# Which experts' first products are formed in blocks in the first batch, and the knobs of a hand-written schedule, on one Trainium2 core

## The chip, the core and the metric

The kernel runs on one core of one Trainium2 chip. The metric is the device time of one execution in microseconds (us); the median of several runs counts. A profiled execution has two numbers of its own: its device time, and its span, which goes from the first to the last instruction of the program.

## What is computed

Sliding-window attention with sink tokens is followed by a mixture of four experts over the same tokens. Cut to what matters:

```
q, k, v: [4 batches, 8 heads, 768 tokens, 64]      window 128, 4 sink tokens
a   = softmax(q k^T / 8), kept where key < 4 or 0 <= query - key < 128
x   = (a v), laid out as [3072 tokens, 512]
p   = domain_probs / (sum over experts + 1e-9)      [3072, 4]
out = sum over e of  p[:, e] * (relu(x @ w1[e]) @ w2[e])
w1: [4, 512, 1024]     w2: [4, 1024, 512]
```

## The kernel before

**Tiling.** A group is 256 tokens; each of the four batches has three. (b, g) is group g of batch b. A *unit* (b, g, e) is the first product of one group with one expert: x times w1[e], the relu, and, from (0, 2) on, the gate. A unit is made in one of three ways:

- *Plain* (`emit_first`, matmuls at L1114): four steps of eight matmuls, each 128x128 by 256 columns, so 32 matmuls of 256 columns. A step ends with one operation that takes the relu and writes half a block of H (L1127 on ACT, L1129 on DVE, or L1138 on DVE with the gate).
- *In blocks*, which the code calls fast (`emit_fast`, L1204): a product of 2x2 blocks with seven block products in place of eight (P1 to P7), so 56 matmuls of 128 columns. Its block sums cost ACT two copies of 128x512 (L1250, L1263) and DVE two additions of 128x512 (L1257, L1272) on top of the four relu or gate operations that a plain unit has too.
- *Turned* (`emit_turning`, L1316): the same seven block products with the operands exchanged, 14 matmuls of 512 columns. The result lies the wrong way round and is turned by two DMA transposes into H.

A unit in blocks needs, besides the tokens, four sums of blocks of w1[e] (`weight_form1`, L390 to L396, one DVE operation of 128x1024 each) and four sums of token blocks of its group (`tokens`, L1170). The last of the four weight sums overwrites a block of w1[e], so it waits until no plain unit of that expert is left.

`START` says from which (b, g) on an expert's units are made in blocks: expert 2 always, expert 1 from (0, 2), experts 0 and 3 from (1, 0). So batch 0 has four units in blocks and eight plain ones. The 20 units from (2, 1) on are turned.

The second product is plain for (0, 0) and (0, 1) (`emit_second`, L1575, eight matmuls of 512 columns for 128 tokens and one expert) and in seven block products after that (`emit_product`, L1489), again with sums on DVE (L1430, L1407).

**What sets the order.** All instructions are written out in order by a planner that runs while the program is built. It keeps a clock for each engine (`t["pe"]`, `t["dve"]`, ...) and for the DMA queue, with a cost for each operation. In each round it lists what TensorE could do next (an attention step, a step of an open unit, a second product), when each is ready by these clocks and with which priority, and emits the best. Operations of ACT and DVE are put on a list by `later` with the time at which they are ready and a slack (`MASK`, `FORM`, `TOKEN`, ...); of those that are ready, the one with the earliest deadline is emitted first. So a slack moves an operation in DVE's queue, and any change of a cost or of a readiness can reorder everything that follows.

**Weights, rows and homes.** Weights and the rows of q, k and v come in by DMAs that POOL issues in program order, through one queue. The first ones are written out by hand (L505 to L520); those of experts 1 and 2 are next; when the attention of batch 0 has been emitted, the loads of w1[3], w2[3] and of the rows of batch 1 are appended (L1678 to L1687). The planner starts the weight sums of an expert `MARGIN1` (4000 ns) after its estimate of when w1[e] has landed, and none before `SOON` while only batch 0 is under way (L1708); `next_form` asks for one at a time, experts in the order 0 to 3. Six homes hold H (`NH`); a second product of plain kind frees its home at its end, a product in blocks at its last block. Units of (0, 2) keep theirs until all second products of (0, 0) and (0, 1) are done. At most two units are open at a time (`WIDE`).

Of the kernel before, what the change touches and what calls it, by code (L numbers as in the profile page):

```python
# [12 lines left out]
BF16 = mybir.dt.bfloat16  # L13
# [3 lines left out]
def kernel(  # L17
# [57 lines left out]
    MASK = 5000  # L75
    GATE = 800
    GATE0 = 300
    FORM = 6000
    TOKEN = 3000
# [7 lines left out]
    SCALED = 300  # L87
    SHARED = 2
# [4 lines left out]
    SOON = 34000  # L93
    NEARLY = 2
    ROWED = 24000
    GATED = 38000
    W2AT = 2
# [411 lines left out]
    load_v(0, (2, 3))  # L509
    load_w1(0, 4, [0])  # L510
    load_w1(0, 4, [1])
# [235 lines left out]
    def values(b, hp, g):  # L747
# [6 lines left out]
        for qi in range(2):  # L754
            qb = 2 * g + qi
            terms = []
            c = 0
            for (kb, q0, nq) in GROUPS[g]:
                if q0 <= qb < q0 + nq:
                    terms.append((kb, c + (qb - q0) * P))  # L760
                c += nq * P
            if g > 0:
                nc.tensor.matmul(  # L763
                    od[:, qi], lhsT=sinkA[b][:, (qb - 2) * P:(qb - 1) * P], rhs=vsd[b][:, hp],
                    start=True, stop=False, skip_group_check=True,
                )
                cols += 2 * DX
            for ph in range(2):
                for i, (kb, c) in enumerate(terms):
                    nc.tensor.matmul(  # L770
                        od[:, qi, ph], lhsT=a[:, ph, c:c + P], rhs=vx[kb][:, 2 * hp + ph, 0:DX],
                        start=(g == 0 and i == 0), stop=(i == len(terms) - 1), skip_group_check=True,
                    )
                    cols += DX + 5
# [174 lines left out]
    NH = 6  # L949
# [6 lines left out]
    class Mixture:  # L956


        def __init__(self):
            self.early = {g: list(range(E)) for g in range(NEARLY)}  # L960
            self.open = []
            self.units = []
            for b, g in PAIRS:
                fast = [e for e in EXPERTS.get((b, g), range(E)) if self.is_fast(b, g, e)]
                slow = [e for e in range(E) if e not in fast]
                if b == 0:
                    fast, slow = list(range(E)), []
# [6 lines left out]
            self.turning = set(mine[TURNED_UNITS[0]:len(mine) - TURNED_UNITS[1]])  # L974
            self.gated = [u for u in self.order if u not in self.turning]
# [9 lines left out]
            self.stored, self.homed = [], False  # L985
            self.spare, self.lent = [], {}
# [7 lines left out]
        def room(self):  # L994
            if self.units and self.units[0] in self.turning and self.halves() < 2:
                return False
            return self.spare or self.live < NH
# [14 lines left out]
        def widened(self):  # L1012

            x = sb.tile([P, 2, NHP, S], BF16, name="qkT", tag="qkT", bufs=1)
            x = x.rearrange("p i h n -> p (i h n)")
            n = 2 * QF * 2 * P
            self.spare = [x[:, i * n:(i + 1) * n].rearrange("p (k f t n) -> p k f t n", k=2, f=QF, t=2) for i in range(3)]
            self.rest("onat", 2, 2, t["pe"])
            self.rest("aT", 4, 1, t["pe"])

        def opened(self, b, g, e):

            if self.spare:
                self.H[b, g, e] = self.spare.pop()
                self.lent[b, g, e] = self.H[b, g, e]
            else:
                self.H[b, g, e] = mo.tile([P, 2, QF, 2, P], BF16, name="H", tag="H", bufs=NH)
                self.live += 1
            fast = self.is_fast(b, g, e)
            if (b, g, e) in self.turning:  # L1030
                self.G[b, g, e] = [self.half(), self.half()]

            def complete(at):
                self.H_at[b, g, e] = at
                self.finished.add((b, g, e))
                if (b, g) >= PAIRS[0]:
                    self.waiting.append((b, g, e))
                    load_gates()
                    if not TURNED_UNITS[1] and self.gated[-1] == (b, g, e):
                        self.rest_gates()  # L1040

            self.H_part[b, g, e] = join(4, complete)
            return {"unit": (b, g, e), "fast": fast, "left": list(UNITS) if fast else list(range(QF)), "at": {}}
# [17 lines left out]
        def firsts(self):  # L1061
# [15 lines left out]
            if n < WIDE and self.units and (self.units[0][0] or loaded) and early <= MIX and self.room() and not (early + zero and self.live >= NH - 1):  # L1077
# [68 lines left out]
        def tokens(self):  # L1146
# [13 lines left out]
            B11, B21, B12, B22 = x[:, 1, 0:2], x[:, 1, 2:4], x[:, 0, 0:2], x[:, 0, 2:4]  # L1160
# [5 lines left out]
            self.T[b, g] = {"P1": B11, "P2": B21, "P3": B22, "P4": T[:, 3], "P5": T[:, 0], "P6": T[:, 1], "P7": T[:, 2]}  # L1166
            steps = [(T[:, 0], B12, B11), (T[:, 1], B22, T[:, 0]), (T[:, 2], B22, B12), (T[:, 3], B21, T[:, 1])]

            def run(engine):
                nc.vector.tensor_sub(*steps.pop(0))  # L1170
                done = dve(G, rate=1.92)
# [109 lines left out]
        def emit_turning(self, u, m, ready):  # L1281
            b, g, e = u["unit"]
            H, X, at = self.H[b, g, e], self.G[b, g, e], u["at"]
            n = QF * P
            assert len(own_steps) == 4
            if m in ("P1", "P5"):
                spare = [i for i in range(6) if ring[i] <= ready + 40]
                spare.sort(key=lambda i: (whole[i], ring[i]))
                if m == "P1":
# [5 lines left out]
                    def turned(k):  # L1295
                        def turn(at):
                            nc.sync.dma_start(
                                out=H[:, k].rearrange("c f t n -> c (f t) n"), in_=X[k].rearrange("p f t n -> p (f t n)"), transpose=True,
                            )
                            done = sp(at, issue=1330, takes=1400, turning=True) + LANDS  # L1300
                            self.H_part[b, g, e](done)
                            self.H_part[b, g, e](done)
                            self.resting.append((done, X[k]))
# [83 lines left out]
        def chore(self):  # L1387
# [12 lines left out]
            if self.last:  # L1400
                b, g, e = u = self.last[0]
                if (b, g, "P2") not in self.products:
                    self.last.pop(0)

                    def form(engine):
                        H12 = self.H[b, g, e][:, 1, :, 0]
                        nc.vector.tensor_sub(H12, H12, self.S[b, g][1][:, e])  # L1407
                        self.S4_at[u] = dve(QF * P, rate=1.92)
                    return go(form, self.until(b, g, e, "P3"))
# [9 lines left out]
            self.waiting.pop(0)  # L1419
            if (b, g) not in self.S:  # L1420
                self.S[b, g] = [mo.tile([P, E, QF, P], BF16, name=f"S{i}", tag=f"wide{i}", bufs=1) for i in range(2)]
            H = self.H[b, g, e]
            H11, H21, H22 = H[:, 0, :, 0], H[:, 0, :, 1], H[:, 1, :, 1]
            S = self.S[b, g]
            steps = [(nc.vector.tensor_add, S[0][:, e], H21, H22), (nc.vector.tensor_sub, S[1][:, e], S[0][:, e], H11),
                     (nc.vector.tensor_sub, H21, H11, H21)]

            def form(engine):
                x = steps.pop(0)
                x[0](*x[1:])  # L1430
                at = dve(QF * P, self.stored[-1] if (b, g) == PAIRS[0] else 0.0, rate=1.92)
                if steps:
                    go(form, self.until(b, g, e, "P6 P7".split()[len(steps) == 2]))
                else:
                    self.S_at[u] = at
                    self.last.append(u)
            return go(form, self.until(b, g, e, "P6"))
# [5 lines left out]
        def operand(self, b, g, e, m):  # L1443
            H = self.H[b, g, e]
            if m in ("P5", "P6"):
                return self.S[b, g]["P5 P6".split().index(m)][:, e]
# [23 lines left out]
        def emit_product(self):  # L1470
# [30 lines left out]
            if m == CHAIN[-1]:  # L1501
                if (b, g, e) in self.lent:
                    self.spare.append(self.lent.pop((b, g, e)))
                else:
                    self.live -= 1
# [56 lines left out]
        def emit_second(self):  # L1562
# [35 lines left out]
            if s == 1:  # L1598
                self.live -= 1
# [16 lines left out]
    def own_made():  # L1616
# [13 lines left out]
        later("dve", t["pe"], 5000, run)  # L1630
# [29 lines left out]
    while mix.more() or att.more():  # L1660
# [69 lines left out]
        opts.append((max(p, now), HIGH_PRODUCT if behind > BEHIND or mix.live >= FULL or wide and TURN_ABOUT and mix.turn_about else LOW_PRODUCT, "product", None))  # L1730
# [65 lines left out]
```

## Time and profile before

| | us |
|---|---|
| median of 3 runs | 354.03 (353.99 to 354.43) |
| the profiled execution, its own time | 354.08 |
| its span | 352.37 |
| TensorE's last matmul ends, from the start of the span | 349.20 |
| TensorE busy (matmuls) | 346.4 |
| VectorE (DVE) busy | 284.1 |
| ScalarE (ACT) busy | 207.9 |
| GpSimd (POOL) busy | 73.6 |

TensorE's granted clock is full throughout. Matmuls are pipelined: a matmul's listed duration holds its way through the array, so what it costs in a row of matmuls is the distance from its start to the next start. The chain of work that ended last is 94% TensorE.

### The profile page before, as it was taken

Reading aid. Unit: us, or ns where it says so; the run is one execution under the profiler, and the core shown is the slowest. Engines: PE = TensorE matmul, PEld = TensorE weight load, DVE = VectorE, ACT = ScalarE, POOL = GpSimd, SP = SyncE. Lnnn points to the kernel's source line nnn. Section 1 sums busy time; section 2 is a strip of 40 time slices with the busy share of each in tenths; the row PEclk is TensorE's granted clock in tenths of the full one; section 3 lists DMA queues with packets and bytes.
Section 4 is the critical chain, followed back from the end, with each engine's and each line's share of the span. In section 5 each row is a group of like instructions: output and inputs, shape, how many; then the busy total and the mean of one; then the engine's idle time right before and its main releaser. Section 6 shows DMA issues by size and latency. Waiting matters only on the chain.

```text
span 352.4 us, 9356 instructions
## 1 busy us (share of the span) xinstructions
PE 346.4 (98%) x3722; PEld 266.8 (76%) x3722; DVE 284.1 (81%) x673; ACT 207.9 (59%) x475; POOL 73.6 (21%) x91
## 2 busy tenths in 40 slices
PE   7999999999999999999999999999999999999996
PEld 3685769756789998998999886755856676666685
DVE  6886999978999999799898999578768586675740
ACT  6763723438775443647463439689579767666611
POOL 8966114340442606000152000000000000000000
PEclk9999999999999999999999999999999999999999
DMA  9999999999999999720999513646438743645541
GB/s 178 177 188 195 221 216 180 176 158 178 154 141 133 148 205 110 95 70 6 91 204 169 85 38 55 126 96 121 86 84 166 134 96 91 121 116 111 75 120 61
DMA packets 161032, 45.61 MB, mean 129 GB/s; under 512 B 144740, under 2 KB 156996, under 8 KB 160988
## 3 DMA queue, kind: packets, MB, share of 16 engines
q0 software_dynamic: 79104, 17.31, 56.0%
q1 hardware_dynamic: 80828, 27.18, 42.4%
q8 instruction: 29, 0.48, 0.6%
q10 hardware_dynamic: 1056, 0.52, 0.5%
q14 instruction: 15, 0.12, 0.1%
HBM read 38.39 MB, written 6.34 MB: 127 GB/s over the span
## 4 chain that ended last, share of the span: by engine, by line
PE 94%; DVE 3%; DMA 2%; POOL 0%; issue 0%; ACT 0%; DVEq 0%
PE acc L1489 35%; PE cps L1204 18%; PE cps L1316 17%; PE acc L1575 8%; PE hps L1114 7%; PE sps L704 3%; PE od L770 3%; DMA vx<-in_v_dram 2%; PE od L763 1%; DVE aT L738 1%; DVE T L1170 1%; DVE onat L800 1%; PE tx L834 1%; PE tr L601 0%; PE sinks L665 0%; PE acc L580 0%
## 5 line engine op out<-in xcount | busy, mean ns | idle before, releaser
L1489 PEld LDWEIGHTS <-H 128*128 128x128 bf16 x708 | 66.6, 98 | 17.8 <-issue 1.1
L729 ACT ACTIVATE aT<-sps 128x512 bf16<-128x512 f32 (+1 forms) x96 | 47.2, 579 | 16.7 <-PE sps L704 16.6
L1489 PE MATMUL acc<-w,H 128*128 128x256 bf16 x420 | 56.8, 273 | 0.0
L1204 PEld LDWEIGHTS <-w 128*128 128x128 bf16 x640 | 39.2, 98 | 1.2 <-issue 0.5
L1489 PEld LDWEIGHTS <-S 128*128 128x128 bf16 x320 | 30.4, 98 | 9.4 <-issue 0.8
L1237 DVE SCALAR_TENSOR_TENSOR H<-cps,gates 128x512 bf16<-128x512 f32 x54 | 36.4, 681 | 0.0
L1334 ACT ACTIVATE cps<-cps 128x512 f32<-128x512 f32 x44 | 25.5, 585 | 17.4 <-PE cps L1316 17.0
L1114 PE MATMUL hps<-xT,w 128*128 128x256 bf16 x256 | 31.9, 273 | 0.2 <-DVE H L1129 0.2
L815 ACT ACTIVATE onat<-od,R 128x64 bf16<-128x64 f32 x108 | 24.9, 324 | 11.4 <-DVE R L797 11.1
L315 POOL DMA_DIRECT2D vx<-in_v_dram x24 | 21.4, 898 | 45.1 <-PE od L770 34.0
L1204 PEld LDWEIGHTS <-vf 128*128 128x128 bf16 x480 | 29.3, 98 | 1.0 <-issue 0.5
L1575 PE MATMUL acc<-w,H 128*128 128x512 bf16 x128 | 29.9, 379 | 0.0
L1489 PE MATMUL acc<-wf,H 128*128 128x256 bf16 (+1 forms) x216 | 29.6, 272 | 0.0
L1114 PEld LDWEIGHTS <-w 128*128 128x128 bf16 x256 | 24.2, 98 | 4.9 <-issue 1.1
L1337 ACT ACTIVATE rest<-cps,own_gates 128x512 bf16<-128x512 f32 x37 | 25.5, 693 | 0.7
L723 DVE TENSOR_TENSOR aT<-aT,mask 128x1024 bf16<-128x1024 bf16 (+1 forms) x36 | 22.6, 637 | 3.1 <-ACT aT L729 2.9
L250 POOL DMA_DIRECT2D qkn<-in_q_dram x22 | 19.6, 893 | 25.7 <-DMA qkT<-qkn 18.1
L1204 PE MATMUL cps<-T,w 128*128 128x128 bf16 x320 | 24.3, 219 | 0.0
L1204 PE MATMUL cps<-xT,w 128*128 128x128 bf16 x320 | 24.1, 219 | 0.0
L1316 PE MATMUL cps<-w,T 128*128 128x512 bf16 x80 | 23.8, 379 | 0.0
L1316 PE MATMUL cps<-vf,T 128*128 128x512 bf16 x80 | 23.6, 379 | 0.0
L1550 ACT COPY osb<-acc 128x256 f32<-128x256 f32 x32 | 12.1, 381 | 19.3 <-PE acc L1489 19.1
(145 smaller groups left out, 676.6 us busy)
## 6 DMA issues: line engine op xcount, KB each, us to landing
w<-in_moe_w_dram POOLq DMA_DIRECT2D x6, 1024.0 KB, 18.5
out_dram<-osb SPq DMA_DIRECT2D x16, 256.0 KB
vx<-in_v_dram POOLq DMA_DIRECT2D x24, 128.0 KB, 6.7
qkn<-in_q_dram POOLq DMA_DIRECT2D x22, 128.0 KB, 6.9
qkn<-in_k_dram POOLq DMA_DIRECT2D x22, 128.0 KB, 7.1
gates<-gate_rows SPq DMA_DIRECT2D x20, 128.0 KB
w<-in_moe_w_dram POOLq DMA_DIRECT2D x4, 256.0 KB, 7.4
w<-in_moe_w_dram POOLq DMA_DIRECT2D x2, 512.0 KB, 10.8
```

Of the source, the lines that this page charges most:

```text
L315: nc.gpsimd.dma_start(out=vx[tb][:, :, 0:D], in_=v[b, :, tb * P:(tb + 1) * P, :].rearrange("h p d -> p h d"),)
L723: nc.vector.tensor_mul(a, a, m[:, None, :].to_broadcast([P, 2, w]))
L729: nc.scalar.activation(out=a[:, ph], in_=sps[ph][:, 0:w], func=AF.Exp, scale=scale)
L815: nc.scalar.mul(o[:, qi, hp, ph * D:(ph + 1) * D], od[:, qi, ph, 0:D], R[:, qi, ph])
L1114: nc.tensor.matmul(h[:, i].rearrange("p (q n) -> p q n", q=2), lhsT=w1_sb[e][:, db, fb * P:(fb + 1) * P], rhs=xT[b, g][:, :, db], start=(i ...
L1204: nc.tensor.matmul(y[:, f], lhsT=A[:, d, f * P:(f + 1) * P], rhs=T[:, d], start=(m in ("P1", "P5") and f == 0 and d == 0), stop=(d == 1), ...
L1237: nc.vector.scalar_tensor_tensor(out=dst, in0=src, scalar=0.0, in1=gate, op0=ALU.max, op1=ALU.mult)
L1316: nc.tensor.matmul(y.rearrange("p f n -> p (f n)"), lhsT=T[:, d], rhs=A[:, d], start=(m in ("P1", "P5") and d == 0), stop=(d == 1), skip_g ...
L1334: nc.scalar.activation(out=src, in_=src, func=AF.Relu)
L1337: nc.scalar.mul(X[k][:, :, s], src, gate)
L1489: nc.tensor.matmul(y, lhsT=self.operand(b, g, e, m)[:, f], rhs=forms[e][m][:, f, cs], start=(k == 0 and f == 0 and m in (("P1", "P5", "P2" ...
L1575: nc.tensor.matmul(op, lhsT=H[:, fb // QF, fb % QF, s], rhs=w2_sb[e][:, fb, :], start=(fb == 0), stop=(fb == NFB - 1),)
```

## The change

It does five things.

1. `START`: expert 1's units are in blocks from (1, 0) on, no longer from (0, 2); expert 3's from (0, 0) on, no longer from (1, 0). Batch 0 then has six units in blocks (experts 2 and 3) and six plain ones (experts 0 and 1).
2. The loads: the first quarter of w1[0] goes ahead of the last block of v of group (0, 1); w1[3] goes behind the first row block of batch 1 (`W1AT`).
3. The slacks of masks, weight sums and token sums are shorter, and `SOON` is 24000 in place of 34000.
4. From batch 1 on the two 128-token halves of a group change places in the attention's result, and the first two token sums become one operation of 512 columns.
5. The homes of H are one tile with a list of free places, the oldest first; a turned unit takes its home when its transpose is emitted, and counts against the free ones from when it is opened. The order of the rows in the S tiles is that in which the units are done. Expert gates for the turned units are loaded earlier, for batches 1 to 3, and normalised earlier. Other new names stand at values that switch them off (`EXTRA`, `PROMISED`, `JOIN`, `WAITS` at 0, `ALTER` with 99).

```diff
-    OWN = 2
-    TURNED_UNITS = (4, 0)
+    OWN = 1
+    TURNED_UNITS = (16, 0)
-    START = {0: (1, 0), 1: (0, 2), 2: (0, 0), 3: (1, 0)}
+    START = {0: (1, 0), 1: (1, 0), 2: (0, 0), 3: (0, 0)}
-    MASK = 5000
+    MASK = 4000
-    FORM = 6000
-    TOKEN = 3000
+    FORM = 4500
+    TOKEN = 2000
-    SOON = 34000
+    SOON = 24000
+    W1AT = 1
...
-    load_v(0, (2, 3))
+    load_v(0, (2,))
     load_w1(0, 4, [0])
+    load_v(0, (3,))
     load_w1(0, 4, [1])
...
-                    od[:, qi], lhsT=sinkA[b][...], rhs=vsd[b][:, hp],
+                    od[:, qi ^ (b > 0)], lhsT=sinkA[b][...], rhs=vsd[b][:, hp],
...
+            one, two = (0, 1) if b else (1, 0)
+            B11, B21, B12, B22 = x[:, one, 0:2], x[:, one, 2:4], x[:, two, 0:2], x[:, two, 2:4]
...
+            steps = [(T[:, 2], B22, T[:, 0]), (T[:, 3], B21, T[:, 2])]
+            if b:
+                steps = [(T[:, 0:2], x[:, 1].rearrange(...), x[:, :, 0:2])] + steps
+            else:
+                steps = [(T[:, 0], B12, B11), (T[:, 1], B22, B12)] + steps
...
-            self.spare, self.lent = [], {}
+            self.homes = [mo.tile([P, NH, 2, QF, 2, P], BF16, name="H", tag="H", bufs=1)]
+            self.spare += [(self.homes[0], i) for i in range(NH)]
...
+        def home(self, u):
+            self.lent[u] = x, i = self.spare.pop(0)
+            self.H[u] = x[:, i]
+            self.live += 1
...
             if (b, g, e) in self.turning:
                 self.G[b, g, e] = [self.half(), self.half()]
+                self.promised.append((b, g, e))
+            else:
+                self.home((b, g, e))
...
-            loads.append((load_w1, 3))
             for tb in range(NQB):
+                if tb == W1AT:
+                    loads.append((load_w1, 3))
                 if tb == W2AT:
                     loads.append((load_w2, 3))
                 loads.append((load_nat, 1, tb))
...
         if rowed == 1 and now > GATED:
             rowed = 2
             load_gates()
+            if OWN == 1:
+                own_load()
...
-            if ahead == 1:
+            if ahead == 1 and OWN > 1:
                 own_load()
-            elif ahead == 2:
-                own_made()
+            elif ahead == OWN:
+                own_made(0 if OWN > 1 else 20000)
```

More of the change, by code (lines that the diff above doesn't have):

```diff
@@ L1076, in firsts @@
                 yield at, (OPEN if n else 2), ("early", g)
-            if n < WIDE and self.units and (self.units[0][0] or loaded) and early <= MIX and self.room() and not (early + zero and self.live >= NH - 1):
+            if n < WIDE and self.units and (self.units[0][0] or loaded) and early <= MIX and self.room() and not (early + zero and self.free() <= 1):
                 yield self.unit_ready(*self.units[0], QF), (OPEN if n else 2) - EARLY, ("unit",)
@@ L1296, in turn @@
                         def turn(at):
[L1297 to L1303, printed above, removed]
+                            self.unturned.append(((b, g, e), k, at))
+                            self.turn_rows(True)
                         return join(2, turn)
@@ L1403, in chore @@
                     self.last.pop(0)
+                    us = [u]
+                    if JOIN and self.last and self.last[0][:2] == (b, g) and self.joint([u, self.last[0]]):
+                        us.append(self.last.pop(0))
                     def form(engine):
[L1406 to L1409, printed above, removed]
+                        H12 = self.blocks(us, 1, 0)
+                        nc.vector.tensor_sub(H12, H12, self.rows(us, 1))
+                        at = dve(len(us) * QF * P, rate=1.92)
+                        for x in us:
+                            self.S4_at[x] = at
+                    return go(form, min(self.until(*x, "P3") for x in us))
             if not self.waiting:
@@ L1418, in chore @@
                 return False
-            self.waiting.pop(0)
+            us = [u]
+            if JOIN and len(self.waiting) > 1 and self.waiting[1][:2] == (b, g) and not (
+                self.waiting[1] in self.turning and self.H_at[self.waiting[1]] > max(t["pe"], t["dve"])
+            ) and self.joint([u, self.waiting[1]]):
+                us.append(self.waiting[1])
+            elif JOIN and sum(x[:2] == (b, g) for x in self.row) % 2 == 0 and self.until(b, g, e, "P6") > WAITS:
+                return False
+            del self.waiting[:len(us)]
             if (b, g) not in self.S:
                 self.S[b, g] = [mo.tile([P, E, QF, P], BF16, name=f"S{i}", tag=f"wide{i}", bufs=1) for i in range(2)]
[L1422 to L1425, printed above, removed]
+            n = sum(x[:2] == (b, g) for x in self.row)
+            us.sort(key=lambda x: self.lent[x][1])
+            for i, x in enumerate(us):
+                self.row[x] = n + i
+            H11, H21, H22 = self.blocks(us, 0, 0), self.blocks(us, 0, 1), self.blocks(us, 1, 1)
+            S = [self.rows(us, i) for i in range(2)]
+            steps = [(nc.vector.tensor_add, S[0], H21, H22), (nc.vector.tensor_sub, S[1], S[0], H11),
                      (nc.vector.tensor_sub, H21, H11, H21)]
@@ L1501, in emit_product @@
             if m == CHAIN[-1]:
[L1502 to L1505, printed above, removed]
+                self.release((b, g, e))
+                self.freed_at = end
+                self.turn_rows()
             if k < E - 1:
@@ L1614, in own_load, with own_made @@
         sp()
-    def own_made():
+    def own_made(wait):
         steps = [
```

115 lines of the change are left out of this document (87 added, 28 removed).

## The prediction

> **What bounds the kernel now.** I read the busy slices of the page first:
>
> ```profile
> PE   7999999999999999999999999999999999999996
> DVE  6886999978999999799898999578768586675740
> ```
>
> A slice is 8.8 us. TensorE (PE) is short of full only in the first and the last. The waits of PE by releaser say the same, and give all that there is:
>
> ```profile
> PE acc L580 <- DVE lent L486: 1.4, 1, 1.4
> PE od L770 <- DMA vx<-in_v_dram: 0.4, 1, 0.4
> PE hps L1114 <- DVE H L1129: 0.2, 1, 0.2
> PE tx L834 <- DVE onat L800: 0.2, 1, 0.2
> ```
>
> The last of these ends at 18.5 us. From about 23 to 349.2 us TensorE runs without a wait, so the time is the sum of what its instructions cost, plus a start, plus a tail of 352.37 - 349.20 = 3.2 us that the change doesn't touch. DVE comes next, and stage by stage it is nearer to its limit than its 81% says. By stretches (columns: span, then busy us of PE, PEld, DVE, ACT, POOL):
>
> ```profile
> 55.00:71.00 16.00, 16.00 (x210) 13.20 (x208) 15.04 (x26) 7.77 (x14) 7.01 (x8) 1.00 1.68 173
> 71.00:90.00 19.00, 19.00 (x181) 12.03 (x180) 14.98 (x31) 11.07 (x33) 3.50 (x4) 1.00 1.88 164
> 90.00:140.00 50.00, 50.00 (x715) 45.10 (x712) 49.40 (x123) 28.86 (x84) 22.11 (x26) 1.00 1.60 149
> ```
>
> DVE has 0.96, 4.0 and 0.60 us free in them. The chain of work that ended last gives the price of TensorE's rows (start, us, what):
>
> ```profile
> 14.95 1.52 DVE T L1170 x3
> 16.47 1.34 DVE aT L738 x4
> 17.81 0.60 DVE H L1129
> ...
> 46.55 2.62 PE hps L1114 x24
> 49.17 1.73 PE acc L1575 x8
> ...
> 55.24 8.04 PE cps L1204 x144
> ```
>
> **1. Plain or in blocks: the main term.** 2.62 us for 24 matmuls of 256 columns is 0.109 each, so a plain unit (32) costs 3.49 us. 8.04 us for 144 matmuls of 128 columns is 0.0558 each, so a unit in blocks (56) costs 3.13 us. The difference is 0.37 us. Three units of expert 3 change to blocks and one of expert 1 changes back: 2 x 0.37 = 0.74 us less on TensorE, which has no slack. A unit in blocks can need one extra 512-column matmul (L1212); among the 20 such units no row of that line appears, so I cost it at nothing. If both new units had one, at the 0.216 us per 512 columns of L1575 (1.73 / 8), that would be 0.43 us back.
>
> The Trainium skill speaks against this trade: "TensorE: Matmul & The Clock Gate", section "Back-to-back issue gap", says that in a stream of weight load and matmul pairs a 128-column matmul takes about 81 ns, not 56. By it a unit in blocks would cost an estimated 56 x 81 ns = 4.5 us, and the two added units would lose some 2 us in place of gaining 0.74. The chain's row shows 55.8 ns with a weight load ahead of every matmul, so here the trace decides against the page.
>
> **What comes with it on DVE and ACT.** A unit in blocks adds two DVE additions (L1257 and L1272, 0.69 and 0.68 us listed, 0.60 from start to next start) and two ACT copies (0.59 each). By stretch: 55 to 71 loses the two additions of expert 1's unit in (0, 2) (-1.2), gains the fourth weight sum of expert 3 (+0.6) and the four small operations that normalise the gates (0.19 + 0.24 + 0.23 + 0.21 = +0.9): +0.3 against 0.96 free. 71 to 90 gains 2 x 1.2 = 2.4 against 4.0 free. 90 to 140 gains 1.2 for (0, 2), and loses the weight sum now at 106.3 (-0.6) and the gate operations now at 116.7 (-0.9): -0.3. So all fits beside TensorE's work, narrowly in the first stretch: 0. Were that cover gone, what doesn't fit would come out on TensorE one for one, up to 0.7 us. ACT has 8 us free in each of the first two; its six more copies less two (4 x 0.59 = 2.3 us) are covered.
>
> **2. When expert 3 is ready.** This is where a new wait could arise. Its plain units needed only w1[3]; in blocks they need four weight sums too. The POOL queue's row shows the load (L328) ahead of the row block (L250):
>
> ```profile
> 28.80 0.75 POOL L328 DMA_DIRECT2D w<-in_moe_w_dram  x1 [0.29 <-DMA qkn<-in_k_dram]
> 29.71 0.88 POOL L250 DMA_DIRECT2D qkn<-in_q_dram  x1 [0.16 <-issue]
> 30.59 0.88 POOL L250 DMA_DIRECT2D qkn<-in_k_dram  x1
> ```
>
> By the landings in the trace w1[3] is there at 57.45, and q and k of that block at 58.42 and 59.38. Exchanged, the row block comes first and w1[3] some 1.93 us later, at 59.4; POOL issues the same three instructions, and what is behind them lands as before. The code waits 4.0 us more: 63.4. Now the sums on DVE:
>
> ```profile
> 49.93 0.68 DVE L390 TENSOR_TENSOR vf<-w 128x1024 bf16<-128x1024 bf16 x1
> 52.41 0.68 DVE L392 TENSOR_TENSOR vf<-vf,w 128x1024 bf16<-128x1024 bf16 x1
> 53.13 0.69 DVE L394 TENSOR_TENSOR vf<-w,vf 128x1024 bf16<-128x1024 bf16 x1
> 55.01 0.68 DVE L396 TENSOR_TENSOR w<-w 128x1024 bf16<-128x1024 bf16 x1
> ...
> 63.83 0.68 DVE L390 TENSOR_TENSOR vf<-w 128x1024 bf16<-128x1024 bf16 x1
> ```
>
> Expert 2's four took 5.8 us from first start to last end. Expert 3's would end between 63.4 + 4 x 0.6 = 65.8 (back to back) and 63.4 + 5.8 = 69.2; I take 69.2, the nearest row. TensorE began expert 3 at 63.3 before. What it has in hand without it, from 55.24: expert 1's unit in (0, 2), 3.49; expert 2's three units, 9.4; expert 2's four second products, 4 x 1.73 = 6.9. That is 19.8 us, to 75.0, with homes for it (five of six). 75.0 - 69.2 leaves 5.8 us, so I cost this at 0; past 75.0 each us of delay is a us of TensorE, less the attention of batch 1 that can fill it. That attention's rows land 1.9 us or more earlier for its first block.
>
> **3. The start.** The first quarter of w1[0] passes one block of v, whose landings are 0.7 to 0.8 us apart in the trace (13.49, 14.17): it lands at about 14.6 and not at 15.34, and that v block 1.2 us later (the spacing of the quarters), near 15.4, still ahead of its first reader at 17.2. PE fills 15.70 to 15.93 with two idle products (L580, 0.109 each), so 0.2 us could go to real work. But the chain's rows above show DVE setting the pace there: an earlier first step helps if its relu (0.60 at 17.81) leaves that chain for ACT, a gain of up to 0.6; a mask or relu that gets behind a weight sum now allowed from 24 us loses as much. I take -0.2, by the idle products, and keep -0.6 to +0.6.
>
> **4. Edits with one answer: 0.** The turned units are the same 20 (the last 20 of 36 as of 24). The gates' load grows by half, behind the others on SP, and is read after 210 us. The exchange of halves moves no work; the merged token sum replaces two operations 0.20 apart by one like the 512-column sums of L1430 (0.33 apart): -0.07 us of DVE in nine groups. Homes are as many as before. Switched-off names do nothing. The slacks only reorder DVE. What a new order is worth can't be read from the trace: behind 23 us, PE's starts exceed the usual spacing of their kind by under 2 us in all, most of it around the sinks (L665), so a better order can bring about 1 us at most, a worse one can lose more. I take 0.
>
> **Sum.** 354.08 - 0.74 - 0.2 = 353.14 for an execution like the profiled one, which is 0.05 above the median; I predict **353.1**.
>
> **The rivals.**
> - *The new order also recovers lost PE time.* The start holds 13 idle products after 5 us (1.4 us) and the three short waits (0.8), and the rest under 1 us. Half of that is some 1.1: 352.0. For it: the early weight sums use DVE gaps of 0.9 us between the evacuations at 28 to 34 us. Against: the start hangs on DVE, whose work there is the same.
> - *The gain is given back on DVE.* In the stretch from 90 to 140 DVE has 0.6 us free in 50. If the sums of (0, 2) fall there without the relief that I counted, 0.7 us returns: 353.8. For it: DVE at 99%. Against: the relief of 0.9 is two rows of that stretch.
> - *Expert 3 comes late: slower.* It decides when the fourth weight sum ends after 75.0. That needs 5.8 us more: for instance the sums queued behind second-product evacuations and the relus of three units in a DVE that is 94% busy there. Ending at 77.5, TensorE would stand for 2.5 us, less nothing if batch 1's attention starts at 77.5 as before: 353.1 + 2.5 = 355.6. For it: DVE's 0.96 us of room. Against: the room of 5.8 us, and weight sums are asked for before others.
> - *The change doesn't save what it says.* If a 128-column matmul took its weight load's 98 ns (LDWEIGHTS rows of L1204) in place of 55.8, a unit in blocks would cost 5.49, and two more of them 4.0: 357.9 with the start's 0.2. Twenty units in the trace speak against it. The Trainium skill's 81 ns, named above, is this rival in a milder form.
>
> **Chances.** The forecast's own case 0.45 (352.7 to 353.7, so 0.35 of it is over 0.2% faster); recovery 0.19; given back 0.14; late 0.20; unhidden loads 0.02. 0.2% of 354.03 is 0.71 us, about what a measurement here tells from no change: faster means under 353.32, slower over 354.74. Faster 0.35 + 0.19 = 0.54; same 0.10 + 0.14 = 0.24; slower 0.22. The range runs from 351.9, the recovery case, to 355.1, which takes in the start's loss and the milder part of the late case and leaves out the rest of it (0.13), the unhidden loads and the tails.
>
> **What will show it.** L1114 falls from 256 to 192 matmuls and L1204 rises from 1120 to 1232, at 0.109 and 0.056 apart. The last sum of expert 3 (L396's counterpart) ends before 71 us, and PE has no wait between 55 and 90. PE's last matmul ends near 348.3. The forecast is wrong if PE's rows show waits on weight sums or on H after 60 us, or if DVE's busy share from 90 to 140 doesn't fall and PE's work there stretches.

## The result, and the profile after

The changed kernel takes 355.32 us (355.12 to 355.52), the kernel before 354.01 on the same chip: ratio 1.0034, 95% interval 1.0024 to 1.0044. It is slower by 0.34%, 1.3 us. I had forecast 353.1, within 351.9 to 355.1, so sign and range were both wrong.

The profiled execution took 355.30 us, with a span of 353.60; TensorE's last matmul ends at 350.40, before at 349.20. The same two rows of slices as before:

```profile
PE   8999999999999999999999999999999999999996
DVE  6897989999899999799898989678768586675740
```

TensorE still looks full between the first slice and the last. A slice of 8.8 us at "9" may hide 0.8 us, and here it does. First the part that went as planned. The groups of the page show the exchange of units (192 matmuls of 256 columns in place of 256; weight loads, one for each matmul, of 704 + 528 = 1232 blocks in place of 1120):

```profile
L1177 PE MATMUL hps<-xT,w 128*128 128x256 bf16 x192 | 23.3, 273 | 0.1
...
L1273 PEld LDWEIGHTS <-w 128*128 128x128 bf16 x704 | 43.3, 98 | 2.4 <-issue 1.0
...
L1273 PEld LDWEIGHTS <-vf 128*128 128x128 bf16 x528 | 32.3, 98 | 1.0 <-issue 0.3
```

and the chain that ended last (start, us, what) shows their unchanged prices, 2.62 / 24 = 0.109 and 3.57 / 64 = 0.0558:

```profile
46.99 2.62 PE hps L1177 x24
...
120.43 3.57 PE cps L1273 x64
```

To see where the time went I took from the trace the distance from each matmul's start to the next one's, less the usual distance of its kind (0.0558 us for 128 columns, 0.109 for 256, 0.216 for 512); the few missing records are counted by the written order. What is over is TensorE time lost, counted from the first matmul at 1.40 us. In us, by stretches of the span:

| kernel | work at usual distances | lost 0-24 | 24-60 | 60-112 | 112-140 | 140-end |
|---|---|---|---|---|---|---|
| before | 334.63 | 6.34 | 0.77 | 2.44 | 0.54 | 2.90 |
| after | 333.68 | 7.00 | 0.77 | 3.92 | 0.44 | 3.02 |
| difference | -0.95 | +0.66 | 0 | +1.48 | -0.10 | +0.12 |

The work fell by 0.74 for the two units, as forecast, and by 0.21 for two idle products fewer. Two other stretches took 2.1 us: the start, and 60 to 112 us, where the third group of batch 0 ends and batch 1's attention begins. In the second, five distances are over 0.14 us longer than usual, and none was before: at 63.43 a block product waits 0.26 for DVE's addition (L1326); at 82.80 and 82.98 the scores wait 0.16 and 0.33 for an exp on ACT (L736) to free their bank; at 99.89 a product with v waits 0.19 for a mask on DVE (L730); at 107.71 one waits 0.33 for ACT's L822. That is 1.27 of the 1.48. Two more visits to the scores (TensorE goes over to the matmuls of q k^T and back, at a price that the last section gives) add 0.43, and two shorter waits of the kernel before, 0.25 together, are gone. For the first of the five, these are DVE's rows, then the matmul that waited for the last of them:

```profile
61.68 0.68 DVE L365 TENSOR_TENSOR wf<-wf,w 128x1024 bf16<-128x1024 bf16 x1
62.40 0.69 DVE L367 TENSOR_TENSOR wf<-w,wf 128x1024 bf16<-128x1024 bf16 x1
63.01 0.69 DVE L1326 TENSOR_TENSOR cps<-H,cps 128x512 f32<-128x512 f32 x1
...
63.75 0.61 PE L1273 MATMUL cps<-T,w 128*128 128x128 bf16 x8
```

The view of waits counts only time in which no matmul is listed as running, and each is listed for longer than its distance to the next. So it shows one of the five behind 23 us:

```profile
PE od L770 <- ACT onat L822: 0.2, 1, 0.2
```

DVE and ACT, by the three stretches of the prediction (columns as there):

```profile
55.00:71.00 16.00, 15.90 (x204) 13.48 (x201) 15.62 (x28) 5.90 (x11) 5.63 (x7) 1.00 1.46 191
71.00:90.00 19.00, 18.88 (x229) 13.34 (x227) 18.46 (x41) 10.02 (x25) 4.37 (x5) 1.00 2.06 142
90.00:140.00 50.00, 49.82 (x711) 43.32 (x710) 47.62 (x111) 30.18 (x93) 21.38 (x26) 1.00 1.56 163
```

DVE gained 0.58 us of work in the first and 3.5 in the second, and lost 1.8 in the third. I had +0.3, +2.4 and -0.3: signs right, moved work too small. The four sums of expert 3 on DVE (L396 to L402) lie apart, with other work between them:

```profile
67.99 0.68 DVE L396 TENSOR_TENSOR vf<-w 128x1024 bf16<-128x1024 bf16 x1
...
68.71 0.69 DVE L398 TENSOR_TENSOR vf<-vf,w 128x1024 bf16<-128x1024 bf16 x1
...
70.58 0.68 DVE L400 TENSOR_TENSOR vf<-w,vf 128x1024 bf16<-128x1024 bf16 x1
...
74.42 0.68 DVE L402 TENSOR_TENSOR w<-w 128x1024 bf16<-128x1024 bf16 x1
```

They end at 75.10, where I had 69.2 at the latest and 75.0 as the point from which lateness costs. TensorE came to expert 3 at 75.57 and had other work until then: no wait there.

### The profile page after: what moved, and what is told of

Read it like the earlier page. It is cut to its first block, busy times and chain, and to the rows that moved or that the text cites. A ratio compares the mean times of both kernels' runs of the same rounds, so it can differ in the third digit from the quotient of the medians.

```text
span 353.6 us, 9457 instructions
## 1 busy us (share of the span) xinstructions
PE 347.4 (98%) x3768; PEld 267.0 (76%) x3768; DVE 287.4 (81%) x670; ACT 207.6 (59%) x479; POOL 73.0 (21%) x91
## 3 DMA queue, kind: packets, MB, share of 16 engines
HBM read 38.40 MB, written 6.34 MB: 127 GB/s over the span
## 4 chain that ended last, share of the span: by engine, by line
PE 92%; ACT 3%; DVE 2%; DMA 2%; issue 1%; ACTq 0%
PE acc L1586 34%; PE cps L1273 18%; PE cps L1380 17%; PE acc L1671 8%; PE hps L1177 6%; PE sps L711 3%; PE od L777 3%; DMA kraw<-in_k_dram 2%; PE od L770 1%; ACT aT L736 1%; ACT onat L822 1%; DVE onat L807 0%; PE tx L841 0%; ACT qkT L292 0%; DVE cps L1326 0%
## 5 line engine op out<-in xcount | busy, mean ns | idle before, releaser
L1586 PEld LDWEIGHTS <-H 128*128 128x128 bf16 x732 | 68.3, 98 | 18.6 <-issue 1.6
L1586 PE MATMUL acc<-w,H 128*128 128x256 bf16 x432 | 58.7, 273 | 0.0
L736 ACT ACTIVATE aT<-sps 128x512 bf16<-128x512 f32 (+1 forms) x96 | 47.3, 585 | 15.5 <-PE sps L711 15.5
L1273 PEld LDWEIGHTS <-w 128*128 128x128 bf16 x704 | 43.3, 98 | 2.4 <-issue 1.0
L822 ACT ACTIVATE onat<-od,R 128x64 bf16<-128x64 f32 x112 | 26.4, 344 | 13.5 <-DVE R L804 13.5
L1273 PEld LDWEIGHTS <-vf 128*128 128x128 bf16 x528 | 32.3, 98 | 1.0 <-issue 0.3
L1319 ACT COPY cps<-cps 128x512 f32<-128x512 f32 x22 | 13.4, 608 | 27.9 <-PE cps L1273 24.4
L1273 PE MATMUL cps<-T,w 128*128 128x128 bf16 x352 | 26.7, 219 | 0.1
L1273 PE MATMUL cps<-xT,w 128*128 128x128 bf16 x352 | 26.7, 219 | 0.0
L1273 PE MATMUL cps<-T,vf 128*128 128x128 bf16 x352 | 25.7, 219 | 0.0
L730 DVE TENSOR_TENSOR aT<-aT,mask 128x1024 bf16<-128x1024 bf16 (+1 forms) x36 | 22.6, 638 | 3.0 <-ACT aT L736 3.0
L1177 PE MATMUL hps<-xT,w 128*128 128x256 bf16 x192 | 23.3, 273 | 0.1
L1380 PE MATMUL cps<-w,xT 128*128 128x512 bf16 x80 | 23.0, 379 | 0.0
```

Source lines behind the costliest of these rows:

```text
L730: nc.vector.tensor_mul(a, a, m[:, None, :].to_broadcast([P, 2, w]))
L736: nc.scalar.activation(out=a[:, ph], in_=sps[ph][:, 0:w], func=AF.Exp, scale=scale)
L822: nc.scalar.mul(o[:, qi, hp, ph * D:(ph + 1) * D], od[:, qi, ph, 0:D], R[:, qi, ph])
L1177: nc.tensor.matmul(h[:, i].rearrange("p (q n) -> p q n", q=2), lhsT=w1_sb[e][:, db, fb * P:(fb + 1) * P], rhs=xT[b, g][:, :, db], start=(i ...
L1273: nc.tensor.matmul(y[:, f], lhsT=A[:, d, f * P:(f + 1) * P], rhs=T[:, d], start=(m in ("P1", "P5") and f == 0 and d == 0), stop=(d == 1), ...
L1380: nc.tensor.matmul(y.rearrange("p f n -> p (f n)"), lhsT=T[:, d], rhs=A[:, d], start=(m in ("P1", "P5") and d == 0), stop=(d == 1), skip_g ...
```

## The theories and the experiments

*A*: the units save their 0.74, and the order that the planner writes for 60 to 110 us loses 1.5. *B*: the loss is the start's, from the order of the first loads. *C*: it comes from the shorter slacks. *D* (rival to A): more units in blocks crowd DVE and ACT there whatever the order. As runs came in I added *E*: the loss belongs to the particular order, so that small moves bring and take it; *F*: ACT holds the score banks too long; *H*: the place of the tiles in SBUF. Ratios are to the kernel before on the same chip, with 95% intervals; each "lost" is read as in the table above, from the run's one profile.

**START alone, both ways.**

```diff
 after, a_start_old:   START = {0: (1, 0), 1: (0, 2), 2: (0, 0), 3: (1, 0)}
 before, b_start_new:  START = {0: (1, 0), 1: (1, 0), 2: (0, 0), 3: (0, 0)}
```

> The changed kernel with the experts' START as it was (expert 1 in blocks from (0, 2), expert 3 from (1, 0)); all else stays changed. Theory A (the units in blocks save their 0.74 us, and the order that they force between 60 and 110 us loses some 1.5 us in short stalls and extra visits to the scores): it gives the 0.74 back and loses none of the 1.5, so about 355.3 + 0.74 - 1.5 = 354.6, or 354.0 if the start is as before. Theory B (the loss is at the start, from the new order of the first loads, some 0.7 us by 24 us): 355.3 + 0.74 = 356.0 less what A says nothing of. Theory C (the shorter slacks misorder VectorE): stays at 355 or above.

> The kernel before with only the experts' START changed. Theory A: the loss comes with it, 354.0 - 0.74 + 1.5 = 354.8, with the stalls between 60 and 110 us. Theory B: the start is as before and only the saving is left, 354.0 - 0.74 = 353.3. Theory C: the slacks are the old ones, so 353.3 as well.

355.25 (1.0039, 1.0024 to 1.0054) and 355.67 (1.0041, 1.0029 to 1.0053). With the old units and all else new, 60 to 112 loses 2.91, so 1.0 of the loss goes, but so does the saving of 0.74, and the start still loses 7.2 (of its twelve executions two took 356.84 and 357.98). With only the units new the work falls by 0.74 to 333.90, and the stretch loses 4.64. The units pay what I said; what comes with them costs more, and more yet under the old slacks. A and D both stand. B falls as the main cause: the second kernel has the old loads and is as slow.

**The loads and the slacks.**

```diff
 after, a_loads_old:   load_v(0, (2, 3)); load_w1(0, 4, [0])     first loads as before
 after, a_slack_old:   MASK = 5000; FORM = 6000; TOKEN = 3000; SOON = 34000
```

> The changed kernel with the first loads in the old order (both v blocks ahead of the first quarter of w1[0]). Theory B: the 0.7 us at the start come back, 354.6, though two idle products return. Theory A and C: within 0.3 us of the changed kernel, 355.0 to 355.6, unless the order in the middle is re-made by it.

> The changed kernel with the slacks of masks, weight sums and token sums and the earliest time of weight sums as before. Theory C: 353.3 to 354.0. Theory A: still 355 or so, since the order between 60 and 110 us is still made with expert 3 in blocks; more separate visits to the scores (35 for 33) add some 0.4 us. Theory B: 355.3.

355.09 (1.0026, 1.0016 to 1.0036) and 355.76 (1.0045, 1.0033 to 1.0057). With the old loads the start loses 6.7 in place of 7.0, but the two idle products (0.22) are back, and 60 to 112 loses 3.9 as in the changed kernel: B's 354.6 isn't met. The old slacks bring 60 to 112 down to 3.05 and give it back elsewhere (112 to 140: 1.18; the start 7.17), with 0.43 of the saving gone as well: two of the extra 512-column matmuls that the prediction costed at nothing, L1212 in the old kernel, stand in this run. So the slacks together aren't the cause: C falls as put.

**One expert at a time, on the kernel before.**

```diff
 b_e1plain:   START = {0: (1, 0), 1: (1, 0), 2: (0, 0), 3: (1, 0)}
 b_e3blocks:  START = {0: (1, 0), 1: (0, 2), 2: (0, 0), 3: (0, 0)}
```

> The kernel before with only half of the START change: expert 1's unit of (0, 2) plain, expert 3 as before. Its matmuls cost 0.37 us more. If the loss between 60 and 110 us comes with expert 3's units in blocks (theory D), this is 354.1 + 0.4 = 354.5 and the stretch from 60 to 110 is as before; if any re-made order loses about 1.5 us there (theory E, the planner's order is only good where it was fitted), it is 355.5 or more.

> The kernel before with the other half: expert 3's three units in blocks, expert 1 as before. Matmuls cost 3 x 0.37 = 1.1 us less. Theory D: the loss of some 1.9 us between 60 and 112 us is all here: 354.1 - 1.1 + 1.9 to 2.3 = 354.9 to 355.3. Theory E: the same size, since the order is re-made as well. If the loss belonged to expert 1's plain unit, 353.0.

355.42 (1.0033, 1.002 to 1.0045) and 358.27 (1.011, 1.0094 to 1.0127). One unit made plain should cost 0.37; it costs 1.0, with a wait of 0.48 at 102.18 for an exp on ACT (L729), some 40 us behind that unit. Expert 3 in blocks on top of expert 1's loses 17.84 in all against 12.99 (60 to 112: 4.45 for 2.44; 140 to the end: 4.82 for 2.90). Its long waits between 60 and 113 are for DVE (0.56 at 76.92, 0.64 at 109.88, 0.70 at 112.01). Two extra 512-column matmuls (0.43) are in it as well. The first speaks for E. The second has the waits that D names, but both theories had put it at about 355, and it is 3 us over; what sets its size stays open.

**ACT's banks, and w1[3] first.** `SHARED` says from which batch on ACT's scaling (L822) may go to DVE as well; `W1AT = 0` undoes the exchange of w1[3] and the row block.

```diff
 after, a_shared1:  SHARED = 1
 after, a_w1at0:    W1AT = 0
```

> The changed kernel with the scaling of batch 1's attention results allowed on VectorE too, where ScalarE had them alone (SHARED 1). Theory F (ScalarE, 98% busy from 100 to 110 us after the change and 74% before, holds the banks that PE waits for): the waits on ScalarE at 83, 100 and 108 us go, 0.5 to 1.0 us: 354.3 to 354.8. If ScalarE isn't the cause: 355.3 within 0.3.

> The changed kernel with w1[3] loaded ahead of the first row block of batch 1, as before. If expert 3's weight sums come too late (the recorded rival, which decides at 75.0 us; the fourth sum ended at 75.1), they end up to 2 us earlier and 0.3 to 0.5 us come back: 354.9. Theory F: no change, 355.3, since PE has no wait on a weight sum.

356.15 (1.0053, 1.004 to 1.0066) and 356.21 (1.0057, 1.0043 to 1.0071). Relief for ACT takes the two late waits (60 to 112: 2.96), adds 0.65 of work (three extra 512-column matmuls) and loses 1.1 more behind 112; F isn't borne out as a cure. Without the exchange the rows of batch 1 come late (TensorE waits 1.0 at 86.61 for the transposed rows) and 1.08 at 102.82 for a copy on ACT (L1624): the exchange is worth 0.9 in the changed kernel. Expert 3's four sums end at 68.56 there, 6.5 us earlier, and nothing comes back. So the prediction's rival that expert 3 comes late isn't the cause.

**One slack back.**

```diff
-    MASK = 4000
+    MASK = 5000        a_mask5; a_mask5_loads also has the old first loads
```

> The changed kernel with one constant as before: the slack of the masks is 5000 again (MASK). Theory E (nothing in the units in blocks themselves costs the 1.4 us between 60 and 112 us; it is the order that the planner happens to make there, and another order of VectorE's queue loses less): the attention steps of batch 1 fall otherwise, the waits at 99.9 and 107.7 us go, 0.6 to 1.0 us come back: 354.3 to 354.7. Theory D (six units in blocks in batch 0 crowd VectorE and ScalarE whatever the order): 355.3 within 0.3.

> The same with the first loads in the old order too. The ten profiles so far lose 6.3 to 6.7 us of PE's time by 24 us with the old order and 7.0 to 7.2 with the new, against two idle products (0.22 us) fewer. If that is the load order's (theory B, in part), this is 0.3 us under a_mask5: 354.0 to 354.4. If it is chance: as a_mask5.

354.54 (1.0013, 1.0004 to 1.0022) and 354.65 (1.0014, 1.0005 to 1.0022). All units stay as changed, and 0.8 of the 1.3 us is gone: the waits at 99.89 and 107.71 no longer occur, and the stretch loses 3.17. The three at 63 and 83 stay (0.27, 0.16, 0.33; together about the 0.73 that is still over). So E holds for half of the stretch; the other half is taken up again below. One slack back is faster by 0.8, all four back were slower: what a slack is worth depends on the rest. The old loads on top change nothing that a measurement tells. The stretch from 100 to 110 us by engines, in the changed kernel and then in a_mask5:

```profile
100.00:110.00 10.00, 9.82 (x148) 8.73 (x148) 9.66 (x29) 9.75 (x33) 1.91 (x3) 1.00 1.48 138
```

```profile
100.00:110.00 10.00, 10.00 (x152) 8.87 (x150) 10.00 (x27) 8.44 (x29) 1.76 (x2) 1.00 1.23 116
```

In the second DVE is busy without a gap and TensorE loses nothing; in the first DVE has 0.34 us free, ACT is at 9.75, and TensorE waits. So a high share by itself doesn't make TensorE wait.

**Loads alone; all but the bookkeeping undone.**

```diff
 before, b_loads_new:  load_v(0, (2,)); load_w1(0, 4, [0]); load_v(0, (3,))
 after, a_all_old:     START, first loads, slacks as before; W1AT = 0
```

> The kernel before with only the first loads in the new order. Theory B in part: PE loses 7.0 to 7.2 us by 24 us, less 0.22 for two idle products: 354.0 + 0.3 = 354.3 to 354.5, plus what a re-made order may lose behind that. If the load order is worth what the prediction said: 353.8.

> The changed kernel with START, the first loads, the place of w1[3] and the four slacks as before; what stays changed are the halves' exchange with the merged token sum, the homes as one list, the rows of S in the order of the units, and the gates of the turned units loaded and normalised earlier. The prediction costed these at 0: 354.0 within 0.3. Were they the cause, 355.

354.74 (1.0018, 1.0009 to 1.0027) and 354.65 (1.0015, 1.0006 to 1.0024). The new loads alone cost 0.57. In the profiled execution 0.45 of the loss lies behind 60 us, again by a new order, so I read at most the rest, 0.35 by 24 us, as a price of the loads. The second should have equalled the kernel before: its 60 to 112 does (2.52), yet it takes 0.5 us more. Its loads of the start land later, which brought up H.

**The place of the tiles.** For batches 1 to 3 the two gate tiles hold 18 rows in place of 12. They grow by 128 bytes per partition and push all tiles allocated after them. First the kernel before once more, and with an unused tile; then two kernels with the old gate tiles.

```diff
 before_again:               no edit
 before, b_pad:              +    consts.tile([P, 32], FP32, name="unused")
 after, a_all_old_own2:      as a_all_old, and OWN = 2; TURNED_UNITS = (4, 0)
 after, a_mask5_own2:        as a_mask5, and OWN = 2; TURNED_UNITS = (4, 0)
```

> The kernel before, unchanged, once more with a profile of its own. If what PE loses in the first 10 us (3.28 us in the first profile, 3.4 to 3.9 in the others) is chance from execution to execution, this profile may show any value in that range; if it belongs to the kernel, 3.2 to 3.4 again.

> The kernel before with one unused tile of 128 bytes per partition among the constants, which moves the weights and the rows in SBUF by 128 bytes as the larger gate tiles of the changed kernel do; no instruction is added, moved or taken away. Theory H (the 0.4 us that all kernels with the changed structure lose in the first 10 us come from where the first loads lie in SBUF): 354.6, with the first load of v landing near 8.5 us in place of 7.9. Otherwise: 354.1, and it is something else of the structure.

> As a_all_old (354.65 against 354.17), with the gates of the turned units also loaded and normalised as before, so that every tile lies where it lay before. Left are the exchange of halves, the merged token sum, the homes and the rows of S. Theory H: 354.1. If one of those four is what costs: 354.6.

> As a_mask5 (354.54), with the gates of the turned units loaded and normalised as before: four operations of 0.2 us on VectorE stand at about 117 us in place of 66 to 75 us. Their own cost is nil on PE. Theory E (the loss belongs to the order that comes out, and any small edit ahead of 100 us makes another one): 1 us or more is lost, 355.3 to 356, with new waits near 100 us. Theory D (the units in blocks set the loss): 354.5 within 0.3, less 0.4 by theory H.

354.06 (0.9999, 0.999 to 1.0008); 354.53 (1.0015, 1.0006 to 1.0023); 354.34 (1.0006, 0.9997 to 1.0015); 355.70 (1.0048, 1.0035 to 1.006). An unused tile of 128 bytes, with no instruction changed, costs 0.3 to 0.5 us. With the old gate tiles the bookkeeping of parts 4 and 5 is within what a measurement tells. The last kernel is the plainest case of E: besides the old place and a smaller load of gates, four DVE operations of 0.2 us move from 66-75 us to 118 us, and it takes 1.2 us more than a_mask5, with waits of 1.08 at 101.58 and 0.53 at 107.77:

```profile
PE acc L1586 <- ACT acc L1624: 0.9, 1, 0.9
PE cps L1273 <- DVE cps L1326: 0.4, 1, 0.4
PE sps L711 <- ACT aT L736: 0.2, 1, 0.2
```

This kernel also tells more of D. From 63 to 105 us its matmuls stand in the same order as in b_start_new, which shares the units but neither the slacks nor the bookkeeping, and the same long waits come with them (1.08 at 101.61 there):

```profile
PE acc L1489 <- ACT acc L1528: 0.9, 1, 0.9
PE sps L704 <- ACT aT L729: 0.2, 1, 0.2
```

In these two and in a_w1at0, which has the wait of 1.08 too, the waits of the scores at 83 are missing, though all three have the six units in blocks of the changed kernel. So the waits at 83 belong to an order as well, and D falls for them. The wait at 63 is in every kernel in which expert 1's unit of (0, 2) is plain, in b_e1plain too (0.14 at 63.24), and in no other: it goes with that unit, not with expert 3's. The three kernels have expert 3's sums done earlier than the changed one (by 66.7 to 70.2) and lose more in the stretch (4.6 to 5.0). Of the orders tried with these six units none loses less than 2.96 there, against 2.44 before; whether a better one exists isn't shown.

**The best version, and a second size.** The gate tiles go to another pool, ahead of the homes of H, and an unused tile of the old length takes their place; and the kernel before with an unused tile of 256 bytes.

```diff
 after, a_mask5_place (MASK = 5000):
+    own = mo.tile([P, OWNED, E + 1], FP32, name="own", tag="own", bufs=1)
+    own_gates, own_sum = own[:, :, :E], own[:, :, E]
+    consts.tile([P, 60], FP32, name="unused")
 before, b_pad256:
+    consts.tile([P, 64], FP32, name="unused")
```

> The changed kernel with MASK at 5000 (354.54 before, ratio 1.0013), and the tiles put back where they lay before: the two gate tiles that the change makes longer move to the end of another pool, and an unused tile of the old length stands in their place, so that w1[0] and the rows' tiles have the addresses of the kernel before. No instruction is added, and the order is the same. Theory H (the 128 bytes by which the longer gate tiles push everything behind them cost 0.3 to 0.5 us in the landing of the first loads): 354.1, ratio 1.000, the first block of v lands at 7.7 to 8.1 us. Rival (the start's loss lies in the order of the first loads and in chance): 354.5, first v at 8.3 to 8.7. By either, the waits around 63 and 83 us stay.

> The kernel before with an unused tile of 256 bytes per partition among the constants, where the run with 128 bytes gave 354.53, ratio 1.0015. If a shift by any amount costs (the old place happened to be a good one, or the tile itself costs): 354.5 and the first v past 8.2 us. If only places that are odd multiples of 128 bytes off the old one cost: 354.1 and the first v at 7.8 to 8.1.

354.30 (1.0006, 0.9997 to 1.0015) and 354.21 (1.0002, 0.9993 to 1.0011). H holds: an unused tile of 256 bytes costs nothing, so it isn't the tile but a place that is 128 bytes off. The loads of the first four blocks of v show it, from issue to landing; the kernel before, b_pad and b_pad256 in turn:

```profile
DMA to landing us min/median/max: 5.9/6.1/6.3
```

```profile
DMA to landing us min/median/max: 6.3/6.6/6.7
```

```profile
DMA to landing us min/median/max: 5.9/6.1/6.3
```

The median is 6.1 to 6.3 in the ten kernels with the old place or 256 bytes off, 6.5 to 6.8 in the ten that are 128 off (6.8 in the changed kernel). The first cast of k's rows on ACT, which waits for their load, starts at 4.62 to 4.85 in the first ten and at 4.90 to 5.29 in the others. No version beats the kernel before: with one slack and the place mended, the change comes out level with it.

## Why the prediction was wrong

1. **The units: right.** -0.74 to the digit, at 0.109 and 0.0558 us per matmul, without an extra matmul (L1212). That there was none is in part luck: three of the other runs have two or three of them.
2. **"So all fits beside TensorE's work: 0": wrong.** I compared sums of DVE time with free time in stretches of 16 to 50 us. The sums were off by 0.3 to 1.5 us, yet DVE's work still fits each stretch, and TensorE waited all the same. At 63.43 an addition stands behind two sums of weight blocks on DVE, and TensorE waits 0.26; at 83 the scores of batch 1, written behind expert 3's blocks (first at 80.58, before 77.55), come close together, and six exps then run one behind the other on ACT, which I had as free by 8 us there:

```profile
82.44 2.40 ACT L736 ACTIVATE aT<-sps 128x384 bf16<-128x384 f32 x6
```

   Scores wait 0.49 for their banks. TensorE's rows of the scores show it, before (twelve in a row without a wait) and after:

```profile
77.55 0.67 PE L704 MATMUL sps<-qkT 64*128 64x256 bf16 x12
...
82.67 1.01 PE L711 MATMUL sps<-qkT 64*128 64x256 bf16 x8
```

   These three, 0.75, stay when the late ones are cured, with one slack or with relief for ACT. The two at 83 go only in orders that lose more elsewhere.
3. **"What a new order is worth ... I take 0": wrong.** I wrote that a worse order "can lose more" and gave it no price. I also read too little out of the trace: behind 23 us I found under 2 us over the usual spacing, because I took the way into the scores and back as usual. The table has 6.65 behind 24 us, and 21 visits of 0.216 are 4.5 of them. The new order lost 0.5 in two waits at 100 and 108 and some 0.2 in visits to the scores, which one slack takes back (0.78 by time). The runs give the size that an order has here whatever the cause: 0.6 beyond its work for one unit, 1.2 for four small operations moved, about 0.5 for two loads exchanged. A spread of a us is as large as the forecast gain.
4. **The start, -0.2: wrong.** The quarter of w1[0] did come earlier (14.90 for 15.34), yet the first step of a unit starts at 15.95 for 15.93, since the rows come later. "Edits with one answer: 0" failed in one of them: the longer gate tiles, which I priced as a DMA behind others, cost 0.24 to 0.47 us by their place (three pairs of runs; the smallest is at the edge of the noise). The rest of the start's +0.66 is seen only over all 20 profiles, since two of the kernel before already differ by 0.2 in their first 10 us. By 24 us they lose on average 6.5 with the old loads and the old place, 6.8 with the old loads 128 bytes off, 6.7 with the new loads in the old place and 7.0 with both. So the new loads lose 0.2 to 0.3, as much as the two idle products were to bring.
5. **Expert 3's sums: the bound of 69.2 was 5.9 us off.** Four sums among other work took 7.1 us from first start to last end, and began 4.6 us later than taken (w1[3] landed at 60.43, 1.0 of it). My rival's point of 75.0 was met to 0.1, and its time, 355.6, is near the result, but by luck: TensorE didn't wait for the sums, and earlier sums (a_w1at0) brought nothing back.

Summed: -0.95 of work, +0.3 place, some +0.35 else at the start, +0.75 at 63 and 83, +0.75 by the order around 100: +1.2, against 1.23 in the spans. The order is shown as the cause of the part around 100 (one slack takes it back) and of the waits at 83 (other orders with the same units don't have them); the wait at 63 goes with expert 1's plain unit.

## What to carry to other kernels

Where an order is written by a planner and TensorE never waits, a saving of 0.2% is smaller than what an edit may do by reordering (0.5 to 1.2 us of 354 here): price it with a spread of its own, taken from runs that move one small thing. A stretch's busy share doesn't tell whether work fits; look for the operation that TensorE needs next and what stands ahead of it in its queue. And keep the tiles where they were when sizes change, or count the shift as an edit.

## What the runs showed of the hardware

**The place of a tile in SBUF changes how fast the first loads land.** The float32 tiles that take the first rows of q and k, in pieces of 512 bytes, begin at 192000 and 196096 bytes of a partition in the kernel before as it is built, both multiples of 256. At 128 bytes further on, v's loads, issued while those of the rows are under way, land 0.5 us later (6.1 to 6.6), and at 256 bytes they land as before. The same shift moves other tiles too, the bfloat16 rows' and the weights' among them; which of them matters isn't tried apart. The Trainium skill, "DMA: Bandwidth & Descriptors", section "How a descriptor splits into AXI transactions", says that when a descriptor doesn't start at a multiple of 256 bytes, its first transaction starts at the boundary below; by that a piece of 512 bytes, begun 128 bytes off, would take an estimated three transactions in place of two. It tells this of reads; these are writes into SBUF, so the runs agree with the rule in the parity, and that it is the cause is argued, not shown.

**A visit to the scores costs 0.216 us beside their work.** Those are matmuls of 64 rows of the array. From a matmul of full height to a score the distance is 0.096 us over the usual (21 visits before, 23 after, behind 24 us), and back 0.120; from one line's matmuls to another's, both of full height (426 times before), the median is 0. The Trainium skill, "TensorEngine Tiling (Array Packing)", section "Key Properties", says that a change of tiling mode drains the engine; the trace agrees, and the 0.216 is what it costs here. A finer mixing of attention with products costs TensorE directly, with no wait to be seen.
